# Attention and an ELU feed-forward block in fp32: batch 0 in another order, with GpSimd in the weight conversion, and one more Strassen product split a second time

## The chip, the cores and the metric

The kernel runs on one core of a Trainium2 chip. The metric is the device time of one execution in microseconds (us). Before the change it is 747.63 us, the median of three runs (746.75 to 747.82). Profiles are of one execution; its engines are PE (TensorE matmuls), PEld (TensorE weight loads), DVE (VectorE), ACT (ScalarE), POOL (GpSimd) and SP (SyncE, which issues DMAs). The span of the profiled execution is counted from its first instruction.

A difference of 0.2% of the time, about 1.5 us, is about what a measurement of this kernel can tell from no change.

## The reference

For each of 8 batches with 8 heads, 512 tokens, 32 states and width 64:

```python
scores  = x @ state.T / 8;  a  = softmax(scores);   xread = a  @ state
scores2 = state @ x.T / 8;  a2 = softmax(scores2);  sread = a2 @ x
z = concat([xread, sread], tokens).transpose(0, 2, 1, 3).reshape(8 * 544, 512)
h = z @ w_in                        # 512 -> 2048
g = where(h > 0, h, exp(min(h, 0)) - 1)
out = g @ w_out                     # 2048 -> 512
```

`x` and `state` are float32. `w_in` and `w_out` arrive as float64 and are used as float32.

## The kernel before, in words

All matmuls are in fp32, and the profile shows each as two instructions. The token rows of a batch never form `xread`: the kernel makes `M = state * w_in` per head (`make_m`, 64 by 32 pieces into PSUM, copied out by `copy_m`), and `h` is then attention weights times `M` (`ffn1`, 16 blocks `fo` of 128 columns, two 128x128x512 matmuls each). PSUM has eight banks of 128x512. ELU takes a Relu and an Exp on ACT (`exp_part`) and one `scalar_tensor_tensor` on DVE (`max_part`), and leaves `g_all` of 128 x 16 x 512.

**Batch 0** (`first_batch`, L739) runs while the weights arrive. They come in 32 pieces of 512 KB in float64 (16 of `w_in`, 16 of `w_out`), seven ahead (`NRAW`), all on SP's queue. Each is turned into float32 from its high and low 32-bit words by two helpers: `convert_1` (L208) is three ACT instructions of 128x512 (low word scaled with a large bias, bias taken off again, absolute value of the high word), and `convert_2` (L222) is four on DVE: a max/min that holds the value in range, a shift with a mask, a `scalar_tensor_tensor` that puts sign and exponent in, and an add of the low part. The order of everything in batch 0 is written out in `plan` as a string of steps, and `InOrder` keeps every engine to it. Step `w:k.1` is `convert_1` of piece k and `w:k.2` is `convert_2`; `x`/`xc` transpose x on PE and copy it out on ACT; `sc` scores; `mx`, `tr`, `ae`, `tm`, `ps`, `te`, `su`, `pm`, `tt`, `sd` the two softmaxes, of which `ps` and `pm` run on POOL; `sT`/`sTc`/`sr`/`src` the state read; `M`/`Mc` make and copy `M` (for batch 0 in halves of 256 columns); `F`, `R`, `E`, `O` are the first product, ACT's part, DVE's part, and the second product for one `fo` (four 128x128x512 matmuls that accumulate over all 16 `fo`, without Strassen). `Z` steps are idle matmuls on the identity. At the end of the plan the attention of batch 1 is done, with x transposed on PE.

**Batches 1 to 7** (`batch`, L847) take `ffn1` for 16 `fo`, then the second product by Strassen (`Strassen`, L572): seven products P1, P2, P6, P7, P5, P4, P3 in this order, each half in every dimension (256 rows of `g` by 1024 by 256 columns). A product is two pieces of 8 matmuls of 128x128x256. Some products are split a second time (`Second`, L513): seven products of 4 matmuls of 128x128x128, whose results go to two PSUM banks in turn (`x` and `y` in `run`, L546), each added into `o_sb` by DVE or, where `fresh` is set, partly copied by ACT. Since a later product accumulates in the same bank, its first matmul waits until the result two products earlier has been taken out. From batch 2 on P7, P5, P4 and P3 are split; batch 1 splits only P4 and P3, and computes the weight sums of the others on DVE. The sums of `g` blocks that a split product needs (`Second.sums`, L535) are four DVE instructions of 128x512, of which the last overwrites a block inside `run`. The helper calls `after_p1` ... `after_p5` say what DVE and ACT do after each product.

Attention of the next batch (`attention`, L709) is hung into the Strassen steps as `hooks`: scores and softmax after the first piece of P1, the state read seven steps later. It needs the column weights turned and moved (`move_state`, L359): DVE transposes of 32x32 blocks and 16 small DMAs on SP. From the end of batch 0 on, the Tile scheduler may reorder DVE's, ACT's and POOL's instructions when it builds the program; on the chip each engine's own queue is then in order.

Of the kernel before, what the change touches and what calls it, by code (L numbers as in the profile page):

```python
# [25 lines left out]
def kernel(  # L26
# [46 lines left out]
    work = pool("work", NRAW + 4)  # L73
    small = pool("small", 4)
    epool = pool("elu", 3)
# [52 lines left out]

    read = cpool.tile([P, B, G, D], FP32, name="read")

    x_t, st, m_t = {}, {}, {}

    def load_x(b, engines):
        x_t[b] = xpool.tile([P, R, DM], FP32, name="x_sb")
        x_v = x[b].rearrange("h (p r) d -> p r h d", r=R)
        for r in range(R):
            engines[r % len(engines)].dma_start(
                out=x_t[b][:, r].rearrange("p (h d) -> p h d", d=D), in_=x_v[:, r]
            )
# [19 lines left out]
    def turn_blocks(b, m):  # L159

        i, j = divmod(m, 2)
        if j == 0:
            st[b, "xT", i] = work.tile([P, 2, R * P], FP32, tag="w", name="xT_b")
# [5 lines left out]
    def load_states(b0, b1, engines=None):  # L169

        shape = [P, b1 - b0, G, D]
        if b0 == 0:
            raw = cpool.tile(shape, FP32, name="s_first")
# [12 lines left out]
    def turn_states(raw, b0, b1):  # L186
        ps = st["k_ps"] = pair(6)[:, :, : (b1 - b0) * 64].rearrange("p t (b q) -> p t b q", q=64)
# [20 lines left out]
    def convert_1(dst, raw):  # L208
# [3 lines left out]
        lo, hi = low_words(raw), high_words(raw)  # L212

        scalar.activation(
            out=lo.bitcast(FP32), in_=lo, func=AF.Copy, scale=2.0**-29, bias=2.0**23
        )
        scalar.activation(out=lo, in_=lo.bitcast(FP32), func=AF.Copy, bias=-(2.0**23))


        scalar.activation(out=dst, in_=hi.bitcast(FP32), func=AF.Abs)  # L220

    def convert_2(dst, raw):  # L222
        lo, hi = low_words(raw), high_words(raw)
        vector.tensor_scalar(
            out=dst, in0=dst, scalar1=as_float(896 << 20),
            scalar2=as_float((1151 << 20) - 1), op0=ALU.max, op1=ALU.min,
        )

# [31 lines left out]
    def copy_x(b, i):  # L260
        xT = opool.tile([P, 2, R * P], FP32, tag="o", name="xT")
        for j in range(2):
            st[b, 2 * i + j] = xT[:, j]
            scalar.copy(
                out=xT[:, j].rearrange("p (r t q) -> p t r q", t=2, q=64),
                in_=st[b, "xT", i][:, :, j],
            )
# [91 lines left out]
    def move_state(b):  # L359
# [7 lines left out]
        for m in range(NP):  # L367
            for q in range(P // 32):
                sync.dma_start(
# [20 lines left out]
    def keep_read(b):  # L390
        for g in range(G):
            scalar.activation(
                out=read[:, b, g], in_=st[b, "sr"][:, g, :D], func=AF.Copy,
# [3 lines left out]
    def turn_read():  # L397

        ps = pair(6).rearrange("p t (b q) -> p t b q", q=64)
        for b in range(B):  # L400
            transpose(ps[:, :, b], read[:, b].rearrange("p g d -> p (g d)"))
# [16 lines left out]
    def make_m(b, c, h=None, first=6):  # L418
# [4 lines left out]
        st[b, "m", c] = by_state(b, [w_in[:, halves, m] for m in range(NP)], first)  # L423

    def copy_m(b, c, g, copy):
        if g == 0:
            m_t[b, c] = mpool.tile([P, G, 512], FP32, name="m_sb")
        copy(out=m_t[b, c][:, g], in_=st[b, "m", c][:, g])

    def copy_half(b, c, h):  # L430
        if h == 0:
            m_t[b, c] = mpool.tile([P, G, 512], FP32, name="m_sb")
        scalar.copy(
            out=m_t[b, c][:, :, h * 256 : (h + 1) * 256], in_=st[b, "m", c][:, :, :256]
# [78 lines left out]
    class Second:  # L513
# [3 lines left out]
        def __init__(self, t):  # L517
            self.t = t

        def weights(self, b):  # L520
# [3 lines left out]
            t1, t2, t4 = (self.t[:, i] for i in range(3))  # L524
# [10 lines left out]
        def sums(self, a):  # L535
# [5 lines left out]
            s1, s2, s3, s4 = s[:, 0], s[:, 1], self.a21, self.a12  # L541
            combine([s1], [self.a21], [self.a22], ALU.add)
            combine([s2, s3], [s1, self.a11], [self.a11, self.a21])
            self.s = {1: s1, 2: s2, 3: s3, 4: s4}

        def run(self, x, y, out, fresh=False):  # L546

            t, s = self.t_w, self.s
            for n, (ps, a, b, first, last, h, c) in enumerate((
# [19 lines left out]
                if n == 1:  # L569
                    combine([s[4]], [self.a12], [s[2]])  # L570

    class Strassen:  # L572
# [36 lines left out]
        def steps(self):  # L609
# [21 lines left out]
            def after_p1():  # L631
                self.copy(0, 0, 0)

# [6 lines left out]
            def after_p6():  # L640
                self.copy(0, 1, 0)
                if 5 in two:
                    self.copy(0, 0, 1)
# [4 lines left out]
            def after_p7():  # L648
                if 7 in two:
                    c21, c22 = self.part(1, 0), self.part(1, 1)  # L650
                    vector.tensor_tensor(out=c21, in0=c21, in1=c22, op=ALU.add)
# [25 lines left out]
            product(0, self.a11, b11, after_p1, first=True)  # L677
            product(1, self.a12, b21, after_p2, first=True, last=True)
            product(0, self.s, t_w[2], after_p6, last=5 in two)
# [16 lines left out]
    shape = [P, 3, FO // 4, P]  # L696
    t_2 = w_in[:, FC:].rearrange("p a b c -> p (a b c)")
    t_2 = [
        t_2[:, k * 3 * DM : (k + 1) * 3 * DM].rearrange("p (i k q) -> p i k q", i=3, q=P)
# [249 lines left out]
```

## Time and profile before

| what | value |
|---|---|
| median of 3 runs | 747.63 us (746.75 to 747.82) |
| the profiled execution's own time | 746.17 us |
| its span | 744.4 us |
| PE busy | 723.7 us (97%) |
| DVE busy | 486.0 us (65%) |
| ACT busy | 293.3 us (39%) |
| POOL busy | 34.4 us (5%) |
| batch 0's first `F` / batch 1's first matmul of `ffn1` / batch 2's / batch 3's | 31.96 / 128.72 / 213.84 / 293.45 us |

The page of a profile gives busy time of each engine over the span, then 40 slices of it, the chain of work that ended last, and groups of instructions. Busy time is an average over stages with different limits, so a table of stretches is read beside it: each of its rows gives, for one stretch of the span, the busy time of each engine with the number of instructions in parentheses, the granted clock of PE, the share of DMA and GB/s. A row of the timeline has start, duration, engine, line, operation, output<-input with shapes and, in brackets, how long the engine stood idle ahead of it and what ended that. Here all lines are L100, because one helper records every operation, so rows are told apart by their tiles: `raw`, `w_in` and `w_out` for the conversion, `s` for sums, `o_sb` for results, `a_s` and `t_sb` for attention.

### The profile page before, as it was taken

The numbers are of one execution on the slowest core, as the hardware profiler recorded it, in microseconds if no ns is written. First come the engines' busy times: TensorE is split into PE (matmuls) and PEld (weight loads), VectorE is DVE, ScalarE is ACT, GpSimd is POOL, SyncE is SP. The second block draws the span as 40 slices with busy tenths as digits, with TensorE's granted clock in tenths as the row PEclk, the third lists the DMA queues.
The fourth block names the chain that finished last, engine by engine and source line by source line (L and its number), as shares of the span: only waits on it lengthen the run. The fifth ranks groups of instructions, "written<-read, shape, count | busy, mean of one in ns | idle before, by whom it ended". The sixth has DMA issues, their size and how long they took to land.

```text
span 744.4 us, 11377 instructions
## 1 busy us (share of the span) xinstructions
PE 723.7 (97%) x4472; PEld 502.5 (68%) x4472; DVE 486.0 (65%) x892; ACT 293.3 (39%) x539; POOL 34.4 (5%) x38
## 2 busy tenths in 40 slices
PE   4899999989999999999999999999999999999998
PEld 2544444348874798469944896479746894699886
DVE  2999975799437883677556864787367845556231
ACT  5899955542126311651055203621264106400420
POOL 0100002002000200010000200020002000000000
PEclk9999999999999999999999999999999999999999
DMA  9667900801634063503461164307340403003000
GB/s 282 225 201 239 326 0 1 167 4 22 177 94 133 5 179 84 160 1 106 122 153 46 26 173 110 116 13 187 83 144 1 143 33 137 1 1 142 29 4 25
DMA packets 126366, 76.25 MB, mean 102 GB/s; under 512 B 113768, under 2 KB 114280, under 8 KB 122472
## 3 DMA queue, kind: packets, MB, share of 16 engines
q1 hardware_dynamic: 124004, 74.90, 34.8%
q10 hardware_dynamic: 2308, 0.62, 0.4%
q8 instruction: 35, 0.57, 0.3%
q14 instruction: 19, 0.16, 0.1%
HBM read 59.24 MB, written 13.11 MB: 97 GB/s over the span
## 4 chain that ended last, share of the span: by engine, by line
PE 89%; DVE 6%; SPq 1%; DMA 1%; ACT 1%; issue 1%; POOL 0%; ACTq 0%; DVEq 0%; POOLq 0%
PE ps L100 89%; DVE w_in L100 2%; SPq L100 1%; DMA x_sb<-in_x_dram 1%; DVE g_all L100 1%; DVE total_t L100 0%; DVE s L100 0%; DVE top L100 0%; DVE w_out L100 0%; ACT e_sb L100 0%; POOL t_sb L100 0%; ACT xT L100 0%; DVE xT_b L100 0%; DVE aT L100 0%; DVE t_sb L100 0%
## 5 line engine op out<-in xcount | busy, mean ns | idle before, releaser
L100 PE MATMUL ps<-w_out,g_all 128*128 128x256 f32 (+2 forms) x1088 | 232.5, 366 | 1.1 <-DVE g_all L100 0.8
L100 PE MATMUL ps<-aT,m_sb 128*128 128x512 f32 x512 | 226.3, 595 | 1.1 <-DVE m_sb L100 0.8
L100 PEld LDWEIGHTS ps<-w_out,g_all 128*128 128x128 f32 x1088 | 176.6, 191 | 53.5 <-issue 37.1
L100 PEld LDWEIGHTS ps<-aT,m_sb 128*128 128x128 f32 x512 | 95.4, 190 | 122.0 <-issue 109.1
L100 ACT ACTIVATE e_sb<-ps 128x512 f32<-128x512 f32 (+1 forms) x144 | 82.5, 573 | 220.4 <-PE ps L100 205.1
L100 DVE SCALAR_TENSOR_TENSOR g_all<-e_sb,ps 128x512 f32<-128x512 f32 (+1 forms) x144 | 94.2, 656 | 101.0 <-ACT e_sb L100 100.4
L100 DVE TENSOR_TENSOR o_sb<-o_sb,ps 128x128 f32<-128x128 f32 (+2 forms) x170 | 52.6, 310 | 75.2 <-PE ps L100 73.5
L100 ACT ACTIVATE e_sb<-e_sb 128x512 f32<-128x512 f32 (+1 forms) x144 | 87.3, 606 | 4.6
L100 PE MATMUL ps<-t_w,s 128*128 128x256 f32 (+1 forms) x480 | 88.8, 339 | 0.0
L100 PEld LDWEIGHTS ps<-t_w,s 128*128 128x128 f32 x480 | 77.6, 191 | 8.1 <-DVE o_sb L100 0.2
L100 ACT COPY o_sb<-ps 128x512 f32<-128x512 f32 (+2 forms) x52 | 20.6, 424 | 151.7 <-PE ps L100 144.6
L100 ACT ACTIVATE raw<-raw 128x512 f32<-128x512 uint32 x64 | 43.7, 683 | 1.0
L100 DVE TENSOR_TENSOR s<-s,g_all 128x512 f32<-128x512 f32 (+1 forms) x36 | 32.2, 897 | 15.9 <-PE ps L100 15.5
L100 POOL TENSOR_TENSOR t_sb<-t_sb,top_t 128x512 f32<-128x512 f32 x16 | 16.7, 1047 | 517.0 <-DVE top_t L100 517.0
L100 DVE TENSOR_TENSOR g_all<-g_all,s 128x512 f32<-128x512 f32 (+1 forms) x36 | 32.1, 891 | 9.6 <-PE ps L100 9.6
L100 PE MATMUL ps<-w_in,kT 64*32 64x512 f32 (+1 forms) x576 | 34.0, 547 | 0.9 <-ACT a_s L100 0.9
L100 DVE TENSOR_TENSOR g_all<-g_all 128x512 f32<-128x512 f32 (+1 forms) x36 | 32.2, 894 | 0.5
L100 DVE TENSOR_TENSOR s<-g_all 128x512 f32<-128x512 f32 (+1 forms) x36 | 31.6, 883 | 0.8 <-DMA aT_s<-a_blocks 0.4
L100 PE MATMUL ps<-t_w,g_all 128*128 128x128 f32 (+1 forms) x240 | 32.1, 282 | 0.0
L100 PE MATMUL ps<-w_in,s 128*128 128x128 f32 x240 | 31.2, 277 | 0.0
L100 PEld LDWEIGHTS ps<-t_w,g_all 128*128 128x128 f32 x240 | 29.8, 192 | 0.5
L100 PEld LDWEIGHTS ps<-w_in,s 128*128 128x128 f32 x240 | 28.7, 192 | 0.6 <-DVE o_sb L100 0.5
(86 smaller groups left out, 557.1 us busy)
## 6 DMA issues: line engine op xcount, KB each, us to landing
w_in<-w_in_mem SPq DMA_DIRECT2D x26, 1024.0 KB, 5.9
raw<-in_moe_w_in_dram SPq DMA_DIRECT2D x16, 512.0 KB, 4.6
raw<-in_moe_w_out_dram SPq DMA_DIRECT2D x16, 512.0 KB, 4.5
out_dram<-o_sb SPq DMA_DIRECT2D x16, 512.0 KB, 2.8
x_sb<-in_x_dram SPq DMA_DIRECT2D x30, 256.0 KB, 4.9
x_blocks<-in_x_dram SPq DMA_DIRECT2D x96, 64.0 KB, 2.4
w_in_mem<-w_in SPq DMA_DIRECT2D x4, 1024.0 KB, 8.3
aT_s<-a_blocks SPq DMA_DIRECT2D x96, 32.0 KB, 1.9
```

Source lines behind the costliest of these rows:

```text
L100: ins = getattr(self.engine, name)(*args, **kw)
```

## The change

**Weight conversion.** `convert_1` and `convert_2` become steps 0, 1 and 2. For pieces with an even number (`held`) the max/min runs on POOL (`w:k.0`), ACT keeps its three instructions, and DVE is left with three. For odd pieces POOL takes the bias off the low word, ACT is left with two instructions and DVE keeps four.

**Batch 0's order.** A new `plan`. x is loaded in two halves of the heads, so eight DMAs instead of four on two queues; its copies are shared by ACT (`xc`) and DVE (`xd`). Pieces come in the order 4 of `w_in`, 4 of `w_out`, and so on. The remaining states are fetched after piece 4 instead of 12 and turned before the first `F` (`kU`, `kUc`). `M` of chunks 2 and 3 is made in one go instead of in halves. Batch 1's x is turned by DVE from blocks (`bt`) instead of by PE, its column weights are moved by DMA (`ab`) instead of by PE, and its state read moves into batch 1, behind which batch 2's x is loaded.

**Second product.** From batch 2 on P6 is split a second time, into banks 4 and 5 and with a second tile for its sums (`apart`). P1's result is copied to both places by ACT, and P6 is added to one of them by seven DVE additions.

**Elsewhere.** The copies of `M` go to ACT alone (DVE had six of eight in a batch). The 16 DMAs of `move_state` go to SP and ACT in turn. The state read stands after the fifth step instead of the seventh. The pool `elu` has 2 buffers instead of 3, `work` 12 instead of 11.

```diff
-    def convert_1(dst, raw):
...
+    def low_part(raw):
+        lo = low_words(raw)
         scalar.activation(
             out=lo.bitcast(FP32), in_=lo, func=AF.Copy, scale=2.0**-29, bias=2.0**23
         )
...
+    def whole_low(raw, engine):
+        lo = low_words(raw)
+        if engine is scalar:
+            scalar.activation(out=lo, in_=lo.bitcast(FP32), func=AF.Copy, bias=-(2.0**23))
+        else:
+            engine.tensor_scalar(
+                out=lo, in0=lo.bitcast(FP32), scalar1=-(2.0**23), scalar2=None, op0=ALU.add
+            )
...
+    def hold(dst, engine):
+        engine.tensor_scalar(
             out=dst, in0=dst, scalar1=as_float(896 << 20),
             scalar2=as_float((1151 << 20) - 1), op0=ALU.max, op1=ALU.min,
         )
...
+                if step == 0:
+                    hold(dst, gpsimd) if holds else whole_low(raw, gpsimd)
+                elif step == 1:
+                    low_part(raw)
+                    if holds:
+                        whole_low(raw, scalar)
+                    high_part(dst, raw)
+                else:
+                    if not holds:
+                        hold(dst, vector)
+                    join(dst, raw)
+                    fetch()
...
-                sync.dma_start(
+                (sync, scalar)[q % 2].dma_start(
                     out=st[b, "aT_s"][q * 32 : (q + 1) * 32, :, :, m * NS : (m + 1) * NS],
...
             s1, s2, s3, s4 = s[:, 0], s[:, 1], self.a21, self.a12
+            if self.apart:
+                s = work.tile([P, 2, FO // 4, P], FP32, tag="w", name="s_2")
+                s3, s4 = s[:, 0], s[:, 1]
             combine([s1], [self.a21], [self.a22], ALU.add)
             combine([s2, s3], [s1, self.a11], [self.a11, self.a21])
+            if self.apart:
+                combine([s4], [self.a12], [s2])
...
             def after_p1():
                 self.copy(0, 0, 0)
+                if 6 in two:
+                    self.copy(0, 0, 1)
+                    two[6].sums(self.s)
...
             def after_p6():
-                self.copy(0, 1, 0)
-                if 5 in two:
-                    self.copy(0, 0, 1)
+                if 6 not in two:
+                    self.copy(0, 1, 0)
                 combine(self.s, self.s, self.a11, ALU.add)
...
-            product(0, self.a11, b11, after_p1, first=True)
+            product(0, self.a11, b11, after_p1, first=True, last=6 in two)
             product(1, self.a12, b21, after_p2, first=True, last=True)
-            product(0, self.s, t_w[2], after_p6, last=5 in two)
+            if 6 in two:
+                in_two(6, 4, (0, 1), after_p6)
+            else:
+                product(0, self.s, t_w[2], after_p6)
...
-                    copy_m(b, c, g, (scalar.copy, vector.tensor_copy)[g])
+                    copy_m(b, c, g, scalar.copy)
...
-        return [lambda: (s1(), s2()), nop, nop, nop, nop, nop, lambda: (state_read(b), keep_read(b))]
+        return [lambda: (s1(), s2()), nop, nop, nop, lambda: (state_read(b), keep_read(b))]
```

In the built program the changed kernel's DVE queue has, from batch 2 on, between the first reduction over the next batch's scores and P6's first addition into `o_sb`: the attention's instructions, the four sums for P6, two updates `g_all<-g_all,s` of 128x1024, P2's addition of 128x512 and three sums for P7, in this order but for small swaps. Behind P6's first addition stands an `s<-s,g_all` of 128x1024, and then its second addition.

## The prediction

> **What bounds the kernel now.** I read the page first, then a table of stretches with its borders at the first matmul of each batch, then the timeline where an engine is late.
>
> ```profile
> PE 723.7 (97%) x4472; PEld 502.5 (68%) x4472; DVE 486.0 (65%) x892; ACT 293.3 (39%) x539; POOL 34.4 (5%) x38
> ```
>
> ```profile
> 0.00:31.96 31.96, 18.91 (x210) 14.53 (x210) 18.05 (x38) 22.17 (x40) 5.10 (x10) 1.00 0.79 248
> 31.96:105.50 73.54, 72.74 (x296) 30.50 (x298) 70.30 (x129) 64.72 (x109) 0.00 (x0) 1.00 0.66 214
> 105.50:128.72 23.22, 23.22 (x177) 10.37 (x178) 10.61 (x24) 10.43 (x22) 4.15 (x4) 1.00 0.00 1
> 128.72:213.84 85.12, 82.03 (x481) 57.05 (x480) 63.76 (x103) 26.62 (x47) 4.19 (x4) 1.00 0.37 87
> 213.84:293.45 79.61, 79.61 (x531) 57.63 (x529) 53.17 (x99) 26.52 (x49) 4.19 (x4) 1.00 0.37 100
> ```
>
> PE is the bound, at granted clock 1.00. It stands idle 13.05 us before batch 0's first `F`, 3.09 in batch 1, and not at all in batch 2. While weights convert (until 105.5, where the last piece's add ends) DVE is busy 70.3 of 73.5 us: there it has almost no slack. So the gain can only be PE work that goes away and idle time at the start; anything that makes DVE late costs.
>
> **Batch 0 up to the first F.** Scores start at 13.72 because ACT's first conversion stands between the two pairs of copies of x. Changed, the copies are shared by ACT and DVE with nothing between. The last x matmul wave still waits for x, landed about 8.98; with 0.80 of transposes and one copy of 0.68 the second half of the scores starts near 10.6: -3.1. Then DVE: on the way from the scores to the second `aT` it converts three pieces, 2.33 + 3.05 + 3.02 = 8.4 us. Changed, only two, one without the hold (1.91) and one with (2.33), and the turned states' copy (1.08): 5.3, so -3.1. First `F` at 31.96 - 6.2 = 25.8.
>
> **PE's own work in batch 0.** `M` of chunks 2 and 3 whole: four half-pieces of 0.60 become two of 0.94, -0.5. Batch 1's x not transposed on PE: 2 x 0.64 = -1.3. Column weights not turned on PE: -0.9. States turned earlier: -0.6. State read into batch 1: -1.0. Together -4.3, so with PE never waiting batch 1 would start at 128.72 - 6.2 - 4.3 = 118.2.
>
> **DVE and POOL in batch 0.** Here is what speaks against it:
>
> ```profile
> 23.62 1.59 DVE L100 TENSOR_SCALAR w_in<-w_in 128x512 f32<-128x512 f32 x2
> 23.63 1.30 POOL L100 TENSOR_TENSOR t_sb<-t_sb,total_t 128x512 f32<-128x512 f32 x1 [3.77 <-DVE total L100]
> ...
> 28.27 1.56 DVE L100 TENSOR_SCALAR w_in<-w_in 128x512 f32<-128x512 f32 x2
> 28.50 1.05 POOL L100 TENSOR_TENSOR t_sb<-t_sb,total_t 128x512 f32<-128x512 f32 x1 [3.57 <-DVE total_t L100]
> ```
>
> ```profile
> 176.62 1.05 POOL L100 TENSOR_TENSOR t_sb<-t_sb,total_t 128x512 f32<-128x512 f32 x1 [1.69 <-DVE total_t L100]
> 176.98 1.24 DVE L100 TENSOR_TENSOR t<-t_w,t 128x512 f32<-128x512 f32 x1
> ```
>
> The hold and the shift take 0.88 together elsewhere; beside POOL 1.59 and 1.56, and both times they end 0.28 us after POOL does. An addition of two SBUF tiles (0.69 elsewhere) takes 1.24 and ends 0.55 after POOL. So these DVE instructions wait until POOL's is done, with 0.15 to 0.2 of their own start hidden. Beside POOL at 118.23 an ELU step that reads PSUM keeps its 0.69, and reductions keep 0.68. All four conversion steps on DVE are of the first kind.
>
> After its `F` DVE had 28 conversions of 2.33 (65.2) and 14 ELU steps of 0.69 (9.7): 74.9 in 70.3 busy, as neighbours overlap (0.94). Changed: 15 of 2.33, 15 of 1.91 and 9.7 make 73.3, times 0.94 = 68.9. Into that fall 29 of the 32 new POOL instructions. No row has a POOL `tensor_scalar` of 512. From below: `MEMSET` 0.10 for one element and 0.20 for 128, so 0.50 for 512. From above: 1.05 for the two inputs. Between: the one-input `AFFINE_SELECT`, 0.29 for 128, 0.87 for 512. I take 0.7. DVE then loses 0.7 - 0.2 = 0.5 each, in the 87% of its time that is conversion: 29 x 0.5 x 0.87 = 12.6, which uses up the 3.2 of idle. The last add ends at 25.8 + 68.9 + 12.6 = 107.3; with 23.2 behind it as before, batch 1 starts at 130.5, **+1.8** against 128.72. Bounds: 0.50 gives 7.6 lost and -3.2; 1.05 gives 21.4 and +10.6; no loss gives 25.8 + 72.1 + 23.2 = 121.1, -7.6.
>
> The Trainium skill's GPSIMD Engine Reference (3.1 Elementwise — side-by-side cycle accounting) puts bodies of up to two operations at 1.03 cycles per element, and (1. Specifications) the clock at 1.2 GHz: an estimate of 0.44 us for 512 elements, which no run here shows; it speaks for the change. Its 4.1 Engine selection advises VectorE for elementwise work on a tile, which speaks against it. By it batch 0 would come out near -4.7 instead of +1.8.
>
> **Batch 1.** Both waits of PE there are on DVE: 0.76 on an `m_sb` copy, 2.32 on `xT_b`. DVE loses four `M` copies of 0.68 ahead of them to ACT, which was busy 12.8 of 26 us there. -3.1, plus the state read 1.0: **-2.1**. Should they stay, +1.0. P6's weight sums (four of 0.69 on DVE) lie under Strassen, where DVE has slack.
>
> **P6, batches 2 to 6.** The rows of batch 2:
>
> ```profile
> 248.14 0.69 DVE L100 TENSOR_REDUCE top<-ps 128x1 f32<-128x512 f32 x1 [1.17 <-PE ps L100]
> ...
> 255.79 0.71 DVE L100 STREAM_TRANSPOSE aT<-t_sb 128x512 f32<-128x512 f32 x1 [0.56 <-POOL t_sb L100]
> ...
> 258.53 0.71 DVE L100 STREAM_TRANSPOSE aT<-t_sb 128x512 f32<-128x512 f32 x1 [0.65 <-POOL t_sb L100]
> ...
> 260.13 7.07 PE L100 MATMUL ps<-t_w,s 128*128 128x256 f32 x32
> ...
> 262.80 1.22 DVE L100 TENSOR_TENSOR g_all<-g_all,s 128x1024 f32<-128x1024 f32 x1
> 265.52 1.23 DVE L100 TENSOR_TENSOR s<-s,g_all 128x1024 f32<-128x1024 f32 x1 [1.50 <-PE ps L100]
> ```
>
> P6 is 32 instructions of 0.216, 6.91 us until 267.04. Split it is 56 of 0.1116 (rows of eight start 0.893 apart): 6.25, **-0.66**. But DVE, which had nothing to do for P6 while it ran, must now take out every result, in its queue's order. It has worked without a pause from 248.14 to 264.02, 15.88 us with 1.21 of short waits for POOL, on the attention, P7's sums, two updates of `g_all` and P2's addition. In the changed queue the same work stands ahead of P6's first addition, less two `M` copies (2 x 0.61), plus four sums (2.6), plus that addition (0.3). If the sums fill the waits (-1.2): 16.4. The sums meet the second `row_scale` on POOL and wait as above, 0.5: 16.9. PE starts P6 11.99 us after 248.14 and wants the first bank again two products later, at 11.99 + 1.79 = 13.8. It waits 3.1. P6's second addition stands behind a sum of 1.23, so 1.5 later than the first, while PE is 0.89 further: 0.6 more. Net 3.1 + 0.6 - 0.66 = +3.0 a batch, **+15.2** for five. Bounds: waits not filled, and 0.6 again at P7, +4.8 each; all of it hidden, -0.66 each. In batch 7 there is no attention, and only single sums of 0.7 to 1.2 stand ahead of additions: I take **+1** (-0.66 to +2). One more restore (0.69) lies under the state rows' matmuls. ACT's DMA issues and its extra copies lie in its idle time (12.25 us before 267.24); if one was late, P6's addition, which needs P1's copy, would wait behind it.
>
> **Sum:** 1.8 - 2.1 + 15.2 + 1 = +15.9 on the profiled execution's 746.17, so 762.1; the median of the runs is 1.5 above that execution. Forecast **763 us**, slower.
>
> **Rivals.** (1) *Additions in time.* If DVE reaches P6's first addition within 13.8 us of the scores, P6 gains 0.66 six times: 1.8 - 2.1 - 4.0 = -4.3, 743; with batch 0 at -7.6 also, 734. For it speaks that DVE is only 65% busy over the span; against it the unbroken 15.88 us and the queue's order. It decides from a wait of 0.9 us a batch down: below that the whole is faster. Chance 0.13. (2) *POOL's work costs DVE little*, the wait at P6 stays: batch 0 between -7.6 and -4, so 754 to 757. For: short one-input instructions. Against: three rows above. 0.20. (3) *POOL is slow*, at 1.05 or more: batch 0 +10.6, 772 and more, DVE the bound of batch 0. 0.15. The forecast's own case: 0.52 (757 to 768). That the change does not do what it says is excluded by the built program, whose POOL queue holds 32 new instructions and whose P6 is 28 matmuls.
>
> **The numbers.** The range takes in (2) and most of (3) and leaves (1) out: 748 to 780. Faster by over 0.2% (about what a measurement can tell): 0.12, from (1); within: 0.02; slower: 0.86.
>
> **What would show it.** Right: first `F` near 26; POOL `tensor_scalar` near 0.7 and DVE's hold, shift and adds longer beside it; PE waiting for `o_sb` some 3 us in each of batches 2 to 6 at P6's third product; those batches near 82.6 us instead of 79.6. Wrong: batches of 79 us; conversion rows unchanged beside POOL; batch 1 starting near 120.

## The result, and the profile after

The changed kernel takes 785.64 us (median; 784.66 to 786.41) where the kernel before takes 747.73: a ratio of 1.0509, 95% interval 1.0491 to 1.0527. The direction was forecast, the size was not: +37.9 us instead of +15.9, outside the range. The profiled execution has a span of 783.4 us against 744.4.

The page's first line after, and the table of stretches between the first matmuls of the batches (columns: stretch, its length, busy time and instructions of PE, PE's weight loads, DVE, ACT and POOL, PE's granted clock, DMA share, GB/s):

```profile
PE 734.6 (94%) x4540; PEld 510.2 (65%) x4540; DVE 502.6 (64%) x915; ACT 295.8 (38%) x549; POOL 96.6 (12%) x70
```

```profile
27.42:110.00 82.58, 73.39 (x229) 29.08 (x230) 77.59 (x125) 56.48 (x97) 53.78 (x29) 0.98 0.55 153
110.00:138.60 28.60, 25.94 (x92) 9.25 (x91) 13.94 (x30) 8.86 (x18) 4.19 (x4) 0.88 0.47 166
138.60:220.76 82.16, 82.04 (x546) 58.15 (x545) 62.55 (x101) 30.13 (x55) 4.45 (x4) 1.00 0.37 90
220.76:305.20 84.44, 80.98 (x554) 59.54 (x553) 54.46 (x104) 28.88 (x54) 4.47 (x4) 0.98 0.35 94
...
560.62:649.91 89.29, 81.30 (x554) 59.86 (x553) 54.56 (x104) 28.87 (x54) 4.47 (x4) 0.96 0.27 77
```

Read it against the table of before: PE's clock, 1.00 everywhere there, is below 1 in batch 0 and in each of batches 2 to 6, and PE no longer fills those batches. By stage, in us:

| stage | before | after | difference | forecast |
|---|---|---|---|---|
| first `F` | 31.96 | 27.42 | -4.5 | -6.2 |
| start of batch 1 (sum so far) | 128.72 | 138.60 | +9.9 | +1.8 |
| batch 1 | 85.1 | 82.2 | -3.0 | -2.1 |
| batches 2, 3, 4, 5, 6 | 79.6, 79.7, 79.5, 79.7, 80.3 | 84.4, 85.9, 84.7, 84.9, 89.3 | +30.4 | +15.2 |
| batch 7 and the state rows | 131.8 | 133.5 | +1.7 | +1 |

**P6.** PE's timeline in batch 2 of after, and DVE's beside it (start, length, instruction, in brackets the idle time ahead of it and who ended it):

```profile
267.05 1.95 PE L100 MATMUL ps<-t_w,s 128*128 128x128 f32 x16
272.33 1.78 PE L100 MATMUL ps<-w_in,s 128*128 128x128 f32 x8 [3.34 <-DVE o_sb L100]
273.90 1.91 PE L100 MATMUL ps<-t_w,s 128*128 128x128 f32 x8
```

```profile
268.46 0.68 DVE L100 TENSOR_TENSOR s<-g_all 128x512 f32<-128x512 f32 x1
...
270.79 0.68 DVE L100 TENSOR_TENSOR s<-s,g_all 128x512 f32<-128x512 f32 x1
271.39 0.68 DVE L100 TENSOR_TENSOR g_all<-g_all 128x512 f32<-128x512 f32 x1
272.00 0.28 DVE L100 TENSOR_TENSOR o_sb<-o_sb,ps 128x128 f32<-128x128 f32 x1
```

P6's first two products end at 269.0, its third starts 3.34 us later, when DVE has added the first one at 272.00. DVE was never idle; it did P2's addition, an update of `g_all` and P7's three sums first. That is the wait of the forecast (3.1). What the forecast lacks stands in the next rows: eight matmuls of P6 start 0.893 us apart elsewhere, here 1.57, 1.71 and 1.13. The stretches say why (PE's clock is the third figure from the end):

```profile
269.00:272.30 3.30, 0.00 (x0) 0.00 (x0) 3.30 (x7) 0.00 (x0) 0.00 (x0) 1.00 0.96 402
272.30:275.70 3.40, 3.37 (x17) 3.37 (x18) 1.60 (x3) 0.00 (x0) 0.00 (x0) 0.56 0.45 188
```

After the stop the clock is halved. The trace records it at 0.5 for 3.41 us in each of batches 2 to 5 (from 272.69 in batch 2) and for 6.83 in batch 6 (from 614.02), so up to 1.7 and 3.4 us of work are lost. In batches 3 and 6 the stop itself is longer (4.97 and 7.87): there DVE's first sum for P7 waits as well, 1.54 and 4.44 us, for the moves of the probabilities:

```profile
612.84 0.69 DVE L100 TENSOR_TENSOR s<-g_all 128x512 f32<-128x512 f32 x1 [4.44 <-DMA aT_s<-a_blocks]
```

Batches 2 to 6 add up: stops 23.2, low clock 4 x 1.7 + 3.4 = 10.2, PE's work -3.3 (0.66 each, as forecast), together +30.1 of the +30.4.

**Batch 0's end.** ACT, DVE and PE behind the last conversions:

```profile
122.05 5.64 ACTq L100 DMA_DIRECT2D aT_s<-a_blocks  x8
127.74 0.63 ACT L100 ACTIVATE t_sb<-t_sb 128x512 f32<-128x512 f32 x1 [7.35 <-DMA aT_s<-a_blocks]
128.40 0.69 DVE L100 TENSOR_REDUCE total_t<-t_sb 128x16 f32<-128x512 f32 x1 [6.42 <-ACT t_sb L100]
130.21 3.89 PE L100 MATMUL ps<-w_in,kT 64*32 64x512 f32 x30 [2.66 <-DVE t_sb L100]
```

Eight moves of batch 1's probabilities are issued from ACT's queue, 0.7 us each, and the `Exp` that batch 1's tokens need stands behind them. DVE waits 6.42 us, PE 2.66 and then for its clock, at 0.5 from 129.3 to 136.2.

**GpSimd.** Its groups by form (count, busy us, mean ns, idle before):

```profile
L100 POOL TENSOR_SCALAR raw<-raw 128x512 uint32<-128x512 f32 x16 | 27.2, 1707 | 5.3 <-ACT raw L100 4.4
L100 POOL TENSOR_SCALAR w_in<-w_in 128x512 f32<-128x512 f32 x8 | 16.8, 2109 | 18.4 <-ACT w_in L100 15.5 <-DMA x_blocks<-in_x_dram 1.5 <-DVE w_in L100 1.3
```

1.71 us for a low word and 2.11 for a hold, where the forecast took 0.7 and bounded it at 1.05.

### The profile page after: what moved, and what is told of

Its sections match the earlier page's. It is cut to its first block, busy times and chain, and to the rows that moved or that the text cites. A ratio compares the mean times of both kernels' runs of the same rounds, so it can differ in the third digit from the quotient of the medians.

```text
span 783.4 us, 11692 instructions
## 1 busy us (share of the span) xinstructions
PE 734.6 (94%) x4540; PEld 510.2 (65%) x4540; DVE 502.6 (64%) x915; ACT 295.8 (38%) x549; POOL 96.6 (12%) x70
## 4 chain that ended last, share of the span: by engine, by line
PE 73%; DVE 16%; DMA 4%; issue 3%; ACTq 2%; ACT 2%; POOL 1%; DVEq 0%; POOLq 0%
PE ps L100 73%; DVE s L100 4%; DVE w_in L100 3%; DVE w_out L100 3%; ACTq L100 2%; DVE g_all L100 2%; DMA aT_s<-a_blocks 2%; DMA raw<-in_moe_w_in_dram 1%; DVE o_sb L100 1%; DVE top L100 1%; DMA x_sb<-in_x_dram 1%; ACT t_sb L100 1%; DVE t_sb L100 1%; POOL t_sb L100 1%; DMA s_first<-in_state_dram 0%
## 5 line engine op out<-in xcount | busy, mean ns | idle before, releaser
L100 DVE TENSOR_TENSOR o_sb<-o_sb,ps 128x128 f32<-128x128 f32 (+1 forms) x212 | 64.6, 305 | 95.0 <-PE ps L100 92.8
L100 PE MATMUL ps<-t_w,s 128*128 128x128 f32 (+1 forms) x480 | 74.7, 308 | 0.3 <-DVE o_sb L100 0.3
L100 PEld LDWEIGHTS ps<-t_w,s 128*128 128x128 f32 x480 | 68.3, 203 | 3.6 <-DVE o_sb L100 0.7
L100 PE MATMUL ps<-w_in,s 128*128 128x128 f32 x336 | 48.6, 295 | 23.5 <-DVE o_sb L100 23.4
L100 ACT COPY o_sb<-ps 128x128 f32<-128x128 f32 (+2 forms) x46 | 17.7, 401 | 121.4 <-PE ps L100 92.7
L100 PEld LDWEIGHTS ps<-w_in,s 128*128 128x128 f32 x336 | 44.9, 210 | 24.8 <-DVE o_sb L100 24.8
L100 PE MATMUL ps<-w_in,kT 64*32 64x512 f32 (+1 forms) x544 | 37.9, 600 | 6.8 <-DVE w_in L100 4.2
L100 ACT COPY m_sb<-ps 128x512 f32<-128x512 f32 x64 | 33.6, 588 | 11.4 <-PE ps L100 11.4
L100 PE MATMUL ps<-t,s 128*128 128x128 f32 x272 | 35.9, 275 | 0.0
L100 PEld LDWEIGHTS ps<-t,s 128*128 128x128 f32 x272 | 33.2, 192 | 0.0
L100 ACT ACTIVATE raw<-raw 128x512 f32<-128x512 uint32 (+1 forms) x48 | 32.7, 681 | 0.5
```

The lines of the kernel that those rows point to most:

```text
L100: ins = getattr(self.engine, name)(*args, **kw)
```

## The experiments

Theory after the result: three causes, separate. (1) In DVE's queue P6's additions stand behind P7's sums, and the stop also costs PE its clock. (2) ACT's DMA issues hold up batch 0's end. (3) GpSimd's instructions are long and slow DVE beside them. Rivals are in the expectations. Stage lengths are from the profiles, medians from the timed runs; all are edits of the changed kernel.

### e1_p6_whole: P6 not split

```diff
-                product(0, self.s, t_w[2], after_p6)
+                product(0, self.s, t_w[2], after_p6, last=5 in two)
...
-        k: Second(*t_2[3 * i : 3 * i + 3], apart=k == 6) for i, k in enumerate((5, 7, 6, 4, 3))
+        k: Second(*t_2[3 * i : 3 * i + 3], apart=k == 6) for i, k in enumerate((5, 7, 6, 4, 3)) if k != 6
...
-        return [lambda: (s1(), s2()), nop, nop, nop, lambda: (state_read(b), keep_read(b))]
+        return [lambda: (s1(), s2()), nop, nop, nop, nop, nop, lambda: (state_read(b), keep_read(b))]
```

> The changed kernel with P6 multiplied whole again in batches 2 to 6 and 7 (its 32 matmuls, ACT's copies of its result, the read of the state after the first product of P7 as before the change); the new order of batch 0, GpSimd's part of the conversion and all else of the change stay. Theory: the 30.5 us by which batches 2 to 6 grew are P6's: PE waits at P6's third product for DVE's first addition, which stands behind the attention's and P7's sums in DVE's queue, and PE's clock then drops for 3.4 us. Without the split those batches come back to 79.5 to 81 us and the whole to 753 to 757 us. Rival: the batches grew because 8 of the 16 moves of the state's probabilities are issued by ACT and the next x is loaded elsewhere, so DVE and ACT run late whatever P6 does; then batches stay at 83 or more and the whole is at 775 or more.

Measured 756.38 us, ratio to before 1.0113 (1.0091 to 1.0135). Batches 4, 5 and 6 are 80.2, 81.2 and 80.2; PE stops 0.5 (once 1.5) for ACT's copy of P6. So 29 us of the 38 go with P6's split, and the rival falls: the moves are still shared with ACT here. Batch 0 is 110.2 against after's 111.2; e4, e5 and e7, whose batch 0 is the same program too, have 110.2 to 110.3. So what is read from one profile's batch 0 is good to about 1 us.

### e2_no_pool: GpSimd out of the conversion

```diff
-                    hold(dst, gpsimd) if holds else whole_low(raw, gpsimd)
+                    pass
-                    if holds:
-                        whole_low(raw, scalar)
+                    whole_low(raw, scalar)
-                    if not holds:
-                        hold(dst, vector)
+                    hold(dst, vector)
```

> The changed kernel with GpSimd's 32 conversion instructions given back: every low word is made whole by ACT (one more of 0.68 for 16 pieces), every hold is done by DVE (one more of 0.42 for 16 pieces). The order of batch 0 stays. Theory: GpSimd's steps of 1.7 and 2.1 us lie in the chain from a piece's arrival to its last addition and lengthen DVE's steps beside them; the last addition of the conversion comes at 102 to 104 us instead of 109.2, PE's seven waits between 27 and 112 us mostly go, batch 1 starts 5 to 8 us earlier, the whole is at 778 to 781 us. Rival: GpSimd does relieve DVE, and the waits come from the new order (two weight pieces fetched in another order, whole chunks of M waiting for all four of their pieces): then giving the work back costs DVE up to 16 x 0.42 = 6.7 us and the whole is at 786 to 792 us.

Measured 776.48 (1.038, 1.0343 to 1.0417). Batch 0 is 103.5 instead of 111.2, the last addition ends at 103.0 instead of 108.7. Theory holds: DVE does 16 holds more and is done sooner. The median is 1.5 us below the theory's range; batch 5 is 83.3 instead of 84.9, for a reason that e7 takes up.

### e3_moves_on_sp and e6_moves_b1: ACT's issues

e3 issues all moves from SP; e6 only those of batch 1 (`b > 1` keeps the split).

```diff
-                (sync, scalar)[q % 2].dma_start(
+                sync.dma_start(
```

> The changed kernel with all 16 moves of the state's probabilities issued on SP's queue again, as before the change, in batch 0 and in the later ones. Theory: eight issues of 0.65 to 0.7 us each stand on ACT's queue ahead of the Exp that batch 1's tokens wait for; without them PE's 2.7 us of waiting at 130 us and the clock drop behind it go (5 to 6 us), and the moves land earlier in batches 3 and 6, where DVE's sums wait for them (1.5 and 4.4 us and a second clock drop in batch 6: 5 to 8 us); the whole is at 770 to 776 us. Rival: the moves land late because 1 MB fetches of weights and x loads share the DMA engines with them, and SP's queue only puts them further behind: no change or slower, 784 to 790 us.

> The changed kernel with the 16 moves of batch 1's probabilities, at the end of batch 0, all issued by SP; those of the later batches stay shared by SP and ACT. Theory: ACT's queue is what holds up the end of batch 0, and the later batches wait for other reasons that lie in how ACT's issues change the order of DVE's queue; so batch 0 is 6.9 us shorter, as it was with all moves on SP, batch 1 stays at 82.2 us and batches 2 to 6 stay at 84.4 to 89.3: 777 to 781 us. Rival: batch 0's gain is paid back in batch 1, because transfers that follow on SP's queue (the blocks of the next x) land later, as the 90.4 us of batch 1 with all moves on SP may mean: 784 to 788 us.

Measured: e3 768.45 (1.027, 1.0243 to 1.0296), e6 786.56 (1.0527, 1.0505 to 1.0549). In both, batch 0 is 104.3, so ACT's issues cost it 6.9 (5.9 against the 110.2 of e1). But in both batch 1 pays it back: 90.4 and 88.6 instead of 82.2, as e6's rival has it (e3's theory missed that). PE's rows in batch 1 of e6:

```profile
167.94 1.05 PE L100 MATMUL ps<-xT_b,kT 64*32 64x512 f32 x4 [0.77 <-DVE xT_b L100]
171.40 1.06 PE L100 MATMUL ps<-xT_b,kT 64*32 64x512 f32 x2 [2.41 <-DVE xT_b L100]
```

The stop of 2.41 is one that batch 1 had lost by the change (2.32 on `xT_b` in before); the clock is at 0.5 from 171.1 to 174.5 behind it. The stop of 0.77 is new. Before's other stop, 0.76 on `m_sb`, does not come back: the copies of `M` are on ACT in e6 too. DVE's instructions are the same as after's, but in the built queue six sums stand between the second and third transpose of x, and two more ahead of the fourth. And in batches 2 to 6 of e3 (83.7, then 82.0 each) P6's stop is 1.52, not 3.34, again by order; DVE in batch 2 of e3:

```profile
272.19 0.28 DVE L100 TENSOR_TENSOR o_sb<-o_sb,ps 128x128 f32<-128x128 f32 x1
...
277.57 0.69 DVE L100 TENSOR_TENSOR s<-g_all 128x512 f32<-128x512 f32 x1 [1.30 <-PE ps L100]
```

P7's sums now stand behind P6's additions. From batch 1 on DVE's queue is ordered when the program is built. Which queue issues a DMA changed that order here, and with it an engine that the diff did not touch. The stops on the moves in batches 3 and 6 are gone too; why the moves land late there was not tried by itself. Batch 2 is 1.6 us longer than the four behind it though P6's stop is the same. Behind its stop (271.00 to 272.52) the clock is low, behind batch 3's (354.65 to 356.18) it is not:

```profile
273.87:277.28 3.41, 3.41 (x16) 3.41 (x17) 0.43 (x2) 0.00 (x0) 0.00 (x0) 0.50 0.73 204
355.79:359.20 3.41, 2.84 (x23) 2.66 (x24) 2.16 (x6) 0.00 (x0) 0.00 (x0) 1.00 0.34 57
```

### e4_sums_later: P7's sums behind P6

```diff
             def after_p2():
                 self.add(1, 0, 0)
-                combine(self.a12, self.a12, self.s)
-                if 7 in two:
+                if 6 not in two:
+                    combine(self.a12, self.a12, self.s)
+                    if 7 in two:
+                        two[7].sums(self.a21)
+
+            def after_p6():
+                if 6 in two:
                     two[7].sums(self.a21)
...
+                    combine(self.a12, self.a12, self.s)
+                else:
                     self.copy(0, 1, 0)
```

> The changed kernel with P6 still split, but the sums for P7 and the update of the second operand of P2 written behind P6's products instead of behind P2; in the built queue of DVE P6's first addition then stands before 2.6 us of work (0.69 + 0.69 + 1.23) that stood ahead of it. Theory: the wait at P6's third product is the order of DVE's queue; it falls from 3.3 to about 0.7 us, the clock no longer drops, and batches 2, 4 and 5 come to 79.5 to 81 us; 3 and 6 keep the wait for the moves of the state's probabilities (81 to 86). The whole is at 758 to 767 us. Rival: the sums are then missing at P7's third product and the wait only moves there (about 2 to 3 us, with the clock drop): batches of 83 us and more, the whole at 778 or more.

Measured 767.29 (1.0242, 1.0197 to 1.0286). P6's stop is 0.99 to 1.15 in batches 2, 4, 5, which come to 80.7 to 80.9 us; 3 and 6 keep 2.99 and 5.47 (82.7 and 87.0). The clock is low only in batch 6. As the theory says: the same instructions in another order on DVE take most of the stop away.

### e5_fill and e7_fill15: PE kept busy in the stop

```diff
+                if apart and n == 2:
+                    for i in range(28):
+                        matmul(bank(0)[:, :P], ident, ident, start=True, stop=True)
```

e7 has 15 instead of 28.

> The changed kernel with 28 matmuls of the identity by itself (128x128, 0.11 us each by P6's rows, 3.1 us in all; their result is never read) put on PE between P6's second and third product in batches 2 to 7, where PE waits for DVE. They make PE busy in the wait and change nothing else. Theory: after a wait of 3.3 us PE's granted clock is 0.5 for 3.41 us (6.83 us in batch 6), which costs 1.7 us (3.4 us) on top of the wait; kept busy, the clock stays at 1.0 in batches 2, 4 and 5, whose length falls from 84.4, 84.7 and 84.9 to about 82.8 us; in batches 3 and 6 1.9 and 4.8 us of wait are left, and the clock may still fall there; batch 7, whose wait was 0.4, gets 2.7 us longer. The whole at 776 to 782 us. Rival: the low clock in the records costs nothing, and P6's slow rows come from DVE's additions alone; then nothing is won and batch 7 loses 2.7: 787 to 790 us.

> The changed kernel with 15 matmuls of the identity by itself on PE between P6's second and third product. Each became two instructions of 0.1116 us in the run with 28 of them, which so filled 6.25 us and not 3.1; 15 fill 3.35 us, about as long as the wait (3.3 us). Their result is never read. Theory: the clock stays at 1.0 in batches 2, 4 and 5, and what is saved there is the cost of the low clock alone: 1.7 us each, so that they come to 82.7 to 83.3 us instead of 84.4 to 84.9; batches 3 and 6 keep what is over 3.35 us of their waits and come to about 84 and 86 to 88; batch 7 gets 3.0 us longer. The whole at 776 to 781 us. Rival: nothing is saved, since the products run at the pace at which DVE takes them out and not at PE's clock: batches 2, 4 and 5 unchanged, the whole at 787 to 790 us.

e5, 788.03 (1.0545, 1.0521 to 1.057), is inconclusive: its filling ran 6.25 us, twice the stop. e7 gives 775.84 (1.0371, 1.0353 to 1.0389), 10 us less than the change although PE does more:

```profile
268.77 3.51 PE L100 MATMUL ps<-ident 128*128 128x128 f32 x30
272.27 1.16 PE L100 MATMUL ps<-w_in,s 128*128 128x128 f32 x8
273.60 1.16 PE L100 MATMUL ps<-t_w,s 128*128 128x128 f32 x8 [0.17 <-DVE o_sb L100]
```

P6's third product starts at 272.27, as in after, behind the same order of DVE's queue, but at full clock. Batches 2 to 6 come to 83.3, 83.3, 83.4, 83.3 and 84.9: 1.2 to 1.6 us less in 2, 4 and 5 (1.7 of clock; 0.5 of DVE's lateness shows again), 2.6 and 4.4 in 3 and 6, where DVE's waits for the moves were shorter too (a stop of 1.60 is left in 6). The low clock is a cost of its own; the rival falls. Chance says the same twice: in batch 5 of e8, and in batch 5 of e2, the same stop (3.34 and 3.33 us) was not followed by a low clock, and both batches are 83.26, as long as those of e7. The one of e8:

```profile
480.12:563.38 83.26, 79.63 (x554) 58.00 (x553) 54.37 (x104) 28.88 (x54) 4.47 (x4) 1.00 0.36 95
```

### e8_pool_alone, e9_pool_beside, e10_pool_beside_own: GpSimd's price, and who pays it

e8 adds GpSimd instructions at the start, on an unread tile. e9 and e10 take e2 and let GpSimd do the 32 instructions on unread data beside the conversion; e10's edit is shown.

```diff
+        spare = g_all[:, 14:16].rearrange("p k s -> p (k s)")
+        gpsimd.memset(spare, 1.0)
...
+                    if holds:
+                        hold(spare[:, :512], gpsimd)
+                    else:
+                        lo = spare.rearrange("p (j w) -> p j w", w=2)[:, :, 0]
+                        gpsimd.tensor_scalar(
+                            out=lo.bitcast(U32), in0=lo, scalar1=1.0, scalar2=None, op0=ALU.add
+                        )
```

> The changed kernel with eight instructions of GpSimd added at its start, on a tile of its own that nobody reads, while DVE waits for x: twice a tensor_scalar of one operation on 512 contiguous elements, one of two operations, one of one operation on every second word with integers as output, and a tensor_tensor with two inputs. Theory: the 1.71 and 2.09 us of GpSimd's conversion steps are what these instructions take by themselves (a second operation costs 0.4 us), so the same durations show here, beside an idle DVE, and 1.05 for the tensor_tensor. Rival: they are lengthened by DVE's work beside them: then 0.5 to 1.0 us here.

> The kernel without GpSimd in the conversion (all low words by ACT, all holds by DVE), but with 32 instructions of the same two forms on GpSimd, on a tile of its own that nobody reads, so that GpSimd works beside the conversion without being in its chain; all but three of them run one after another from the second row scale on. Theory: GpSimd cost 7.7 us in batch 0 because its 1.7 and 2.1 us stand between ACT's and DVE's steps of each piece; out of the chain its work lengthens only some of DVE's steps by 0.1 to 0.3 us, 2 to 5 us in all: batch 0 at 104 to 108 us, the whole at 777 to 781 us. Rival: DVE waits at each of GpSimd's instructions, as the forecast had it (0.5 us for one of 0.7, and over 1 us for one of 1.9): 25 us and more, the whole at 795 or more. Second rival: DVE loses nothing, the whole as without GpSimd, 773 to 777.

> The last run with GpSimd beside the chain took its unread tile from the rotating buffers of the weight pieces, and a piece's fetch then waited until GpSimd's 32 instructions were over (ACT's conversion stood still for 21.7 us, PE for 27.5 us), which is a fault of that kernel and no answer. Here the same 32 instructions work on two rows of g_all that are written only at the end of batch 0; all else is as there. Theory: out of the chain GpSimd's work lengthens DVE's steps beside it by the 0.1 to 0.2 us each that the rows of that run show (hold 0.54 and 0.49 against 0.42, shift 0.55 and 0.66 against 0.43, the two others 0.75 to 0.83 against 0.69), some 6 to 12 us of DVE's time over 60 us of GpSimd's, of which DVE's idle time covers a part: batch 0 at 106 to 113 us against 103.5 without GpSimd and 111.2 with it, so that the lengthened steps are most of the 7.7 us and the chain little. The whole at 779 to 787 us. Rival: the steps' length in the chain is the cost; then batch 0 stays at 103 to 105 and the whole at 775 to 778 us.

e8 (one run, 787.25), the added groups:

```profile
L100 POOL TENSOR_SCALAR spare<-spare 128x512 f32<-128x512 f32 x4 | 6.8, 1708 | 0.3
L100 POOL TENSOR_SCALAR spare<-spare 128x512 uint32<-128x512 f32 x2 | 3.2, 1592 | 0.2
```

The first group mixes instructions of one operation (1.49 us at the least) and of two (1.93 at the most). So most of the length is GpSimd's own; in the conversion, beside DVE, it is 0.1 to 0.2 more. The `tensor_tensor` there took 1.28.

e9, 813.26 (1.0874, 1.0854 to 1.0895), says nothing: its tile held up a weight buffer. e10, 790.87 (1.0575, 1.0532 to 1.0617): batch 0 is 115.4, 11.9 more than without GpSimd (103.5), though no step waits for GpSimd there. One of DVE's steps, the add, between 28 and 100 us, first of e2, then of e10 (the mean in ns stands after the comma):

```profile
L100 DVE CUSTOM_DVE_ANT_0 w_in<-raw,w_in 128x1024 uint16<-128x1024 uint16 x14 | 9.7, 692 | 0.5
L100 DVE CUSTOM_DVE_ANT_0 w_in<-raw,w_in 128x1024 uint16<-128x1024 uint16 x12 | 9.9, 827 | 0.4
```

The join with sign and exponent goes from 692 to 812, the shift from 427 to 652 and 589, the hold from 420 to 568 and 463; ELU steps, which read PSUM, keep 680. So GpSimd's work slows DVE even where no step waits for GpSimd. For the changed kernel, the stretch from the first `F` to the last addition, first of after, then of e2 (DVE is the third engine of a row):

```profile
27.42:108.70 81.28, 72.09 (x226) 28.51 (x227) 76.35 (x123) 56.48 (x97) 53.78 (x29) 0.98 0.56 155
26.90:103.03 76.13, 72.47 (x231) 29.99 (x232) 73.01 (x139) 67.31 (x115) 0.00 (x0) 0.98 0.62 172
```

DVE is busy 3.3 us longer than in e2 although 16 holds (16 x 0.42 = 6.7) are gone from it, so its other steps are some 10 us longer. Of the 7.7 of batch 0 that leaves 1.8 of idle time of DVE and 2.5 behind the last addition; whether these come from GpSimd's place in the chain of a piece was not tried by itself.

### c1, c8: the rest of the change without its three costs

c1 joins e1, e2 and e3, but leaves batch 2's moves shared. c8 adds DVE's written order for batch 1's sums.

```diff
+        vector.on = b == 1
         whole.sums()
+        vector.on = False
```

(and the same around the four weight sums in `weights`)

> The changed kernel with three parts undone together: P6 whole, no GpSimd in the conversion, and the moves of the probabilities on SP except for batch 2's, which stay shared with ACT. What is left of the change is batch 0's new order and the work that went away in batches 0 and 1. Theory: the three causes are separate and add up. First F at 27, batch 0 at 111.2 - 7.7 - 6.9 = 96.6 us, batch 1 at 82.2, batches 2 to 6 at 79.6 to 80.2, the rest 132.3: a span of 736 to 739.5, the median at 738 to 742 us, faster than before. Rival: the causes overlap at the end of batch 0 (conversion and ACT's queue hide each other), so that only the larger is won, or batch 1 pays 8 us as with all moves on SP: 746 to 752 us.

> The kernel with P6 whole that came to 743.9 us (no GpSimd in the conversion, moves on SP except for batch 2's), with the sums of g_all and the weight sums of batch 1 in written order on DVE, behind the transposes of the next x. Theory: in batch 1 PE loses 5.3 us between the scores and Strassen's first product because these sums, 0.7 to 1.2 us each, overtook the last two transposes; with the order fixed batch 1 comes to 82 to 82.6 us instead of 87.7, and the median to 738 to 740 us. Rival: the transposes are late because their blocks land late, with the moves ahead of them on SP's queue; then batch 1 stays at 86 or more and the median at 742 or more.

c1: 743.85 (0.9952, 0.9934 to 0.997); batch 0 97.3, batches 2 to 6 79.4 to 79.6, but batch 1 87.7 with the two stops on `xT_b`, so its time is between theory and rival. Together the three are worth 41.8 us, less than the sum of 29.3, 9.2 and 17.2 for e1, e2 and e3, since e3 took away part of P6's stops too. c8: **737.66 us, 0.9859 (0.984 to 0.9879), faster than both kernels**:

```profile
26.97:123.86 96.89, 93.23 (x321) 38.07 (x322) 86.08 (x166) 76.46 (x133) 4.19 (x4) 0.98 0.51 140
123.86:206.49 82.63, 82.03 (x545) 58.08 (x544) 59.16 (x96) 30.21 (x55) 4.47 (x4) 1.00 0.51 142
206.49:285.93 79.44, 79.44 (x531) 57.55 (x530) 52.88 (x97) 29.24 (x55) 4.47 (x4) 1.00 0.38 100
```

Batch 1 came back with order alone, and PE fills batch 2 again. Batch 0 from its first `F` on is no shorter than before (96.9 against 96.8); c8's gain lies in the first `F`, 5.0 us earlier, in batch 1 (2.5) and in batches 2 to 6 (1.6 together).

### c5, c7, c9: P6 split, its additions in time

As c1 (c7 and c9: as c8), with P6 split and DVE's order written out by a table of what follows which product:

```diff
+                return {0: half(0), 2: half(1), 4: s7[0], 5: s7[1], 6: s7[2]}
...
+                between.get(n, lambda: None)()
```

c5 orders P6 only, c7 goes on through P7, c9 moves P5's sum ahead of P7's first addition and P4's sums behind its last.

> The changed kernel without GpSimd in the conversion, with the moves on SP except for batch 2's, and with P6 split, but DVE's queue fixed there: P2's addition, P6's seven additions, and between them the two updates of P2's operand (1.21 each) behind the first and the third addition and P7's three sums (0.68 each) behind the fifth, sixth and seventh. Theory: the wait at P6 is only the order of DVE's queue; with it gone P6 gains its 0.66 us of PE work: batches 2 to 6 at 78.9 to 79.5 us, the span at 731 to 736, the median at 733 to 738 us, faster than before and than with P6 whole. Rival: DVE has too little time in Strassen's products for the eight more additions and sums of the split, and the wait moves to P7 or P5: batches of 81 us and more, the median at 744 or more.

> The kernel of the last set with P6 split (no GpSimd in the conversion, moves on SP except for batch 2's), with DVE's order now written out from P2's addition to P7's last product: P6's additions, the two updates of P2's operand behind the first and third, P7's sums behind the fifth to seventh, one half of the sum for P5 between P6 and P7, the other and P5's three second-level sums behind P7's second to fifth products; and in batch 1 the sums of g_all and the weight sums of the second level in written order, behind the transposes of the next x that they had overtaken. Theory: the 1.22 us sum that stood among P6's additions was the whole of its remaining 1.2 us of stops and of the 0.9 at P7; batches 2 to 6 at 78.8 to 79.2 us, batch 1 at 82 to 83 instead of 89.8, the median at 734 to 738 us. Rival: DVE has no room for the eight additions of the split between P2 and P5, and the wait moves to P7 or P5: batches of 80 us and more, the median at 741 or more.

> The kernel with P6 split and DVE's order written out, changed in two places: both halves of the sum for P5 stand ahead of P7's first addition, where DVE waited 1.06 us for PE, and the first sums for P4 stand behind P7's last addition, which they had delayed. Theory: DVE has room for the split, and PE's remaining stop of 0.74 us at P7 was the order alone; P6 and P7 then take 13.0 us together instead of 14.0, batches 2 to 6 come to 79.0 to 79.4 us, against 79.43 with P6 whole, and the median to 737 to 740 us. Rival: DVE is full from P2 to P5, and the wait moves to P5's third product: batches of 80 us and more, the median at 743 or more.

c5 751.62 (1.006, 1.0043 to 1.0077), c7 745.78 (0.9968, 0.9956 to 0.998), c9 743.55 (0.9938, 0.9922 to 0.9954). Batches of 80.9, 80.4 and 79.9 against 79.4 whole. The long stop at P6 is gone in all three; what is left moved: in c5 a sum that was not in the table stood among P6's additions (1.2 us) and 0.72 at P7, in c7 0.74 at P7, in c9 0.24 and short ones at P5. c5's time also holds a batch 1 of 89.8, with a stop of 2.41 as in e6. The theories' 78.8 to 79.5 were never reached, and the medians fell in the rival's range each time. Each mend helped, so order mattered, but no order that I tried makes the split pay.

## Why the prediction was wrong

- **Right: the mechanism at P6 and its size.** 3.1 us of wait forecast, 3.34 to 3.48 measured in batches 2, 4 and 5, at the third product, for the cause named: with P7's sums behind P6 it is 1.0 to 1.15 (e4). The 0.6 more at the fourth product lay under the slow clock and shows in e7 (0.5).
- **Wrong: "Net 3.1 + 0.6 - 0.66 = +3.0 a batch".** The sum lets PE go on at full speed after the wait. The trace of before had no stop of that length in a batch, so no row there shows a clock below 1.00, and I did not ask what a stop costs beyond itself: 10.2 us in five batches. The other 5 of the 15.2 missed there are mainly the longer stops of batches 3 and 6. The Trainium skill's TensorE: Matmul & The Clock Gate (HAM oscillation — how this bites in real kernels) warns of PE gaps over about 3.4 us; the stop of 3.1 forecast was near it. Here 3.34 had the low clock, and once 1.52 had it (e3), so the measurement decides.
- **Wrong: "ACT's DMA issues and its extra copies lie in its idle time".** True by ACT's idle sum, false by its queue. At the end of batch 0 eight issues stood ahead of an `Exp`: the 23.2 behind the last addition became 29.9. That is 6.7 of the 8.1 by which batch 0 was missed; e3 and e6 measured 6.9 (5.9 against e1). The 23.2 "as before" was itself 2 us too long: part of the forecast's own -4.3 of PE work lies behind the last addition, where c8 needs 21.2 (102.64 to 123.86, PE busy throughout). In batch 2 the issues made P1's copies late (266.78; before 254.41), as the forecast's last sentence there allowed, but P6's addition at 272.00 did not wait for them. The stops on the moves in batches 3 and 6 (1.5 and 4.4, in 6 with twice the low clock) went in e3 and stayed in e6, so they come with sharing the later batches' moves; by which way is open.
- **Mis-sized twice, right by luck: "0.7 - 0.2 = 0.5 each ... = 12.6".** GpSimd's instruction takes 1.7 to 2.1, above the upper bound; the nearest rows were of other operations. But DVE loses not its whole length, only a part: in e10 its busy time in batch 0 is 12.5 us above e2's for 29 such instructions, 0.43 each. The last addition came at 108.7, forecast 107.3, so the two errors cancelled. By the forecast's own rule at 1.85 us it would have been 29 x 1.65 x 0.87 = 41.6.
- **First `F`**: 27.42 instead of 25.8. In e1 and e3 to e7, which are the same program up to there, it is 27.5 to 28.5; in the six kernels without GpSimd's conversion (e2, c1, c5, c7, c8, c9) 26.5 to 27.0. So 0.4 us or more of the 1.6 is GpSimd's; what the rest is was not looked for.
- **Batch 1**: -3.0 for -2.1; both waits went, as forecast. The longer one, 2.32 on `xT_b`, went by the order of DVE's queue (c8), not by the four copies moved to ACT: e6 has those copies on ACT too, and a stop of 2.41. The shorter one, 0.76 on an `m_sb` copy, is gone in e6 as well, which fits the forecast's reason; that was not tried by itself.
- The range left out the two together: a stop that costs more than itself, and a queue that blocks. Rival (3) had its size for batch 0 by another cause.

## What to carry to other kernels

Price a new wait of the bounding engine as wait plus what its clock loses afterwards, and look for an order that avoids it before counting the work saved. A DMA issue moved to a compute engine's queue is an instruction there: name what stands behind it. And where a scheduler orders a queue, compare the built order of every engine: a DMA's queue changed DVE's order in two places, for the better in one and the worse in the other.

## What the runs showed of the hardware that was not expected

- The trace's stretches at clock 0.5 are 3.41 or 6.83 us long (one of 27.3 in e9, over a stop of 27.5) and start a whole number of 3.41 us apart (in after at 272.69, 358.02, 443.35 and 528.68, each 25 of them apart). So the length of a stop alone does not say whether one follows: the stop of 3.3 us was in nearly every batch, but not in batch 5 of e2 and e8; one of 1.87 us was (in after, 0.50 from 98.6 to 102.0), one of 2.36 was in e1 (0.50 from 35.0 to 38.5) and not in after; of the five of 1.5 in e3 only that in batch 2 was. The Trainium skill's TensorE: Matmul & The Clock Gate (What's actually happening) has a free-running window of 3.41 us, which agrees.
- What decides in these traces is how much of one such window is without PE work. In e3's batch 2 the window 270.46 to 273.87 has PE busy for 1.71 of 3.41 us, and the next is low; in batch 3 the same stop lies across two windows, busy 2.27 and 2.84, and none is. Over all seventeen traces, from 10 us on, each of the 54 windows at full clock with 1.96 us or more without PE work was followed by a low one, 10 of the 22 with 1.70 to 1.95, and none of the 3332 with less. In two runs the stop of 3.3 us fell so that neither of its windows reached 1.96.
- The kernel before is not free of it: of 45 timed runs of it, 14 have a mean clock of 1.000 (median 746.4 us), 18 of 0.998 (748.2) and 13 of 0.995 (748.5). The profiled execution is one of the first kind, so its rows could not show this.
- GpSimd alone: 1.49 us for one operation on 512 elements, 1.93 for two. The Trainium skill's GPSIMD Engine Reference (3.1 Elementwise — side-by-side cycle accounting) has one price for up to two operations, by which I estimated 0.44 us; the measurement decides.
- GpSimd working without a pause beside DVE lengthened DVE's steps on operands in SBUF by a tenth to a half (hold 420 to 463, add 692 to 827, shift 427 to 652 ns; e2 to e10), and left those that read PSUM at 680.
